# Attention into a feed-forward block on one core: blocks that follow the batches, and loads moved to GpSimd's queue

## The chip, the cores and the metric

The kernel runs on one core of one Trainium2 chip. The metric is device time in microseconds (us) of one execution. A core has five engines with a queue each: TensorE (PE: matmuls, and PEld for its weight loads), VectorE (DVE), ScalarE (ACT), GpSimd (POOL) and SyncE (SP, which only issues DMAs here). Each engine takes its queue in order.

## The reference

```python
def phi(x):
    proj = np.einsum('bhsd,df->bhsf', x, w_phi)
    proj = proj - np.max(np.abs(proj), axis=-1, keepdims=True)
    return np.concatenate([np.exp(proj), np.exp(-proj)], axis=-1)
q_p, k_p = phi(q), phi(k)                       # q, k, v: 8 batches, 8 heads, 576 tokens, 64
kv = np.einsum('bhsf,bhsd->bhfd', k_p, v)
num = np.einsum('bhsf,bhfd->bhsd', q_p, kv)
den = np.einsum('bhsf,bhf->bhs', q_p, k_p.sum(2))[..., None] + 1e-6
x = (num / den).transpose(0, 2, 1, 3).reshape(8 * 576, 512)
h = x @ w_in                                    # 512 x 2048
out = (h * erf(softplus(h))) @ w_out            # 2048 x 512
```

## The kernel before

The attention is done for pairs of heads, four pairs a batch, 32 in all (`NPAIR`, `B`), in groups of four tiles of 128 tokens (`GT`). A group goes through `k_piece` (projection in `project`, L500, maximum and subtraction on DVE in `front`, L468, Exp on ACT), `t_piece` (q is turned, from pair 8 on by a DMA transpose in `turn`, L566: DVE copies to `pl`, SP issues `plt<-pl`, DVE copies back, ACT takes two Exps), `kv_piece` (L576) and `n_piece` (L607). `n_tile` (L612) divides and writes x as two halves of float16 into a tile `xt`: VectorE makes `xf`, ACT or DVE casts it (`XT_ACT`), and POOL or DVE subtracts to get the low half (L651, `X_POOL`). One `xt` holds two pairs, that is half of a batch's channels.

`x_piece` (L692) then turns `xt` by DMA transposes on SP's queue (L704) into tiles `x` of 256 tokens by 512 channels (named `big` in the profile). The 4608 tokens are cut into 18 blocks of 256 (`TB`, `NBLK`), and since a batch has 576 tokens, most blocks hold parts of two batches: a piece of 128 tokens is often cut in two at the edge of a block. This makes 96 transposes.

The feed-forward part takes a block in two halves of the 2048 hidden columns. `h_chunk` (L764) multiplies `x` by `w_in`, with both in a high and a low float16 half, so three matmuls each; `erf_gate` (L799) runs on ACT and DVE; `o_chunk` (L823) multiplies by `w_out`. The first four blocks (`FIRST`) are taken over the first hidden half and then over the second, with partial sums kept in DRAM (`part`). `load_weight` (L408) brings 32 pieces of the weights (512 KB each) to `big` tiles, from where four DVE operations and one of ACT make the two halves (L427 to L436). `load_pair` (L441) brings q and k of a pair into one of three tiles `ld`. All these loads, `v`, the transposes, the partial sums and the output are issued by SP.

The order of each engine's queue is no loop of the program: every operation is recorded in a `Plan` with an assumed cost, due place and buffers, `Plan.run` (L174) lays them out on the five engines, and each queue is then issued in that order. Where the plan sees PE idle for over 600 ns (`HOLE`) it puts in filler matmuls of a tile `hot` (L958). So a constant or a cost in the plan changes the order on all engines, and what the chip does beside it is settled by semaphores.

## Time and profile before

| | |
|---|---|
| median of 3 runs | 995.19 us (995.09 to 996.29) |
| the profiled execution | 995.3 us, span of its instructions 993.5 us |
| granted TensorE clock | 1.0 |
| PE busy | 982.7 us, 99% of the span |
| ACT, DVE, POOL busy | 667.2, 631.3, 56.2 us |
| DMA | 85.94 MB, of the share below nearly all on the queue of SP |

The page gives the busy time of each engine over the span. Busy time of PE is from the start of a matmul to its modelled end, and matmuls overlap, so a short wait can hide under the end of the one before. The views used below are: the waits (who waited for whom), stretches (busy time of each engine in a window), the timeline (instructions in order of time; an entry of SP is the time in which it issues, and in brackets stands the idle time ahead and what ended it), and the view of one tile.

### The profile page before, as it was taken

The numbers are of one execution on the slowest core, as the hardware profiler recorded it, in microseconds if no ns is written. First come the engines' busy times: TensorE is split into PE (matmuls) and PEld (weight loads), VectorE is DVE, ScalarE is ACT, GpSimd is POOL, SyncE is SP. The second block draws the span as 40 slices with busy tenths as digits, with TensorE's granted clock in tenths as the row PEclk, the third lists the DMA queues.
The fourth block names the chain that finished last, engine by engine and source line by source line (L and its number), as shares of the span: only waits on it lengthen the run. The fifth ranks groups of instructions, "written<-read, shape, count | busy, mean of one in ns | idle before, by whom it ended". The sixth has DMA issues, their size and how long they took to land.

```text
span 993.5 us, 36288 instructions
## 1 busy us (share of the span) xinstructions
PE 982.7 (99%) x16674; PEld 780.1 (79%) x16674; DVE 631.3 (64%) x1140; ACT 667.2 (67%) x930; POOL 56.2 (6%) x70
## 2 busy tenths in 40 slices
PE   9999989999999999999999999999999999999998
PEld 7897678777788878877778887878778887777774
DVE  6999989996487826665627775578737742123322
ACT  7869759877667757667657667666857655566571
POOL 0201330210110100000000000000000000000000
PEclk9999999999999999999999999999999999999999
DMA  7492495553344242141313353224232120000000
GB/s 289 125 300 95 123 234 135 142 159 87 83 117 118 48 78 63 45 115 38 81 26 66 74 109 84 72 71 95 66 63 48 34 61 12 13 23 2 22 13 32
DMA packets 118713, 85.94 MB, mean 86 GB/s; under 512 B 99360, under 2 KB 99488, under 8 KB 118560
## 3 DMA queue, kind: packets, MB, share of 16 engines
q1 hardware_dynamic: 118560, 83.62, 32.9%
q8 instruction: 130, 2.13, 0.9%
q14 instruction: 23, 0.19, 0.1%
HBM read 48.46 MB, written 11.53 MB: 60 GB/s over the span
## 4 chain that ended last, share of the span: by engine, by line
PE 87%; ACT 6%; DVE 4%; DMA 1%; issue 1%; SPq 0%; DVEq 0%; ACTq 0%
PE bank L379 69%; PE bank L389 12%; PE bank L523 5%; ACT big L397 1%; DMA plt<-pl 1%; ACT big L794 1%; DVE m L471 1%; PE bank L554 1%; PE bank L958 1%; ACT gh L818 1%; DVE half L431 1%; ACT big L783 1%; ACT L809 1%; ACT L794 1%; DMA big<-in_moe_w_in_dram 0%
## 5 line engine op out<-in xcount | busy, mean ns | idle before, releaser
L379 PE MATMUL bank<-big,wih 128*64 128x256 f16 x4608 | 390.0, 273 | 2.8 <-DMA big<-xt 2.2
L379 PE MATMUL bank<-big,wil 128*64 128x256 f16 x2304 | 318.8, 273 | 0.2 <-DVE wil L435 0.2
L379 PEld LDWEIGHTS <-wih 128*64 128x64 f16 x4608 | 256.6, 110 | 29.1 <-DMA big<-xt 1.9
L397 ACT ACTIVATE big<-big 128x512 f32<-128x512 f32 x234 | 146.3, 629 | 125.0 <-DVE big L482 67.9
L379 PE MATMUL bank<-wol,gh 128*64 128x512 f16 x1152 | 220.6, 379 | 0.0
L379 PE MATMUL bank<-woh,gl 128*64 128x512 f16 x1152 | 220.4, 379 | 0.0
L379 PE MATMUL bank<-woh,gh 128*64 128x512 f16 x1152 | 220.4, 380 | 0.0
L379 PEld LDWEIGHTS <-gh 128*64 128x64 f16 x2304 | 128.8, 110 | 87.0 <-issue 0.3
L783 ACT ACTIVATE big<-bank 128x512 f32<-128x512 f32 x144 | 84.9, 591 | 146.5 <-PE bank L379 146.3
L815 DVE TENSOR_TENSOR big<-big,big 128x1024 f32<-128x1024 f32 x72 | 85.7, 1224 | 152.6 <-ACT big L811 152.5
L379 PEld LDWEIGHTS <-wil 128*64 128x64 f16 x2304 | 131.4, 110 | 2.2 <-DVE wil L435 0.5
L379 PEld LDWEIGHTS <-gl 128*64 128x64 f16 x1152 | 65.4, 110 | 56.3 <-DVE dn L626 0.2
L819 DVE TENSOR_TENSOR gl<-big,gh 128x1024 f16<-128x1024 f32 x72 | 87.3, 1222 | 23.8 <-ACT gh L818 23.7
L471 DVE TENSOR_REDUCE m<-bank 128x4 f32<-128x512 f32 x144 | 92.6, 681 | 12.6 <-PE bank L523 12.0
L389 PE MATMUL bank<-kv,big 128*64 128x65 f32 x2304 | 84.0, 222 | 0.6 <-DVE kv L600 0.6
L389 PEld LDWEIGHTS bank<-v,big 128*64 128x64 f32 x2016 | 75.1, 137 | 9.3 <-ACT big L397 2.9
L389 PE MATMUL bank<-v,big 128*64 128x65 f32 (+1 forms) x2016 | 80.2, 228 | 2.0 <-ACT big L397 1.8
L389 PEld LDWEIGHTS bank<-kv,big 128*64 128x64 f32 x2304 | 76.8, 138 | 4.1 <-issue 1.2
L818 ACT CAST gh<-big 128x1024 f16<-128x1024 f32 x72 | 74.1, 1037 | 0.2
L794 ACT ACTIVATE big<-big 128x1024 f32<-128x1024 f32 x72 | 72.6, 1049 | 0.4
L856 DVE TENSOR_SCALAR half<-bank 128x512 f32<-128x512 f32 x28 | 19.2, 685 | 58.7 <-PE bank L379 58.7
L571 DVE COPY big<-plt 128x1024 uint16<-128x1024 uint16 x54 | 42.3, 783 | 17.8 <-DMA plt<-pl 17.5
(54 smaller groups left out, 916.0 us busy)
## 6 DMA issues: line engine op xcount, KB each, us to landing
ld<-in_qk_dram SPq DMA_DIRECT2D x31, 576.0 KB, 4.7
out_dram<-half SPq DMA_DIRECT2D x36, 256.0 KB, 2.2
v<-in_vp_dram SPq DMA_DIRECT2D x28, 325.0 KB, 3.8
big<-in_moe_w_in_dram SPq DMA_DIRECT2D x16, 512.0 KB, 6.2
big<-in_moe_w_out_dram SPq DMA_DIRECT2D x16, 512.0 KB, 5.0
part<-half SPq DMA_DIRECT2D x8, 256.0 KB, 3.6
half<-part SPq DMA_DIRECT2D x8, 256.0 KB, 3.2
big<-xt SPq DMA_TRANSPOSE x96, 3.0
```

Source lines behind the costliest of these rows:

```text
L379: nc.tensor.matmul(o[half], a[:, half], b, start=start, stop=stop)
L389: nc.tensor.matmul(o[half], a[:, half], b, start=first and c == 0, stop=last and c == 1)
L397: nc.scalar.activation(out_(), in_(), func, **k)
L471: op(DVE, 600, lambda: nc.vector.tensor_reduce(m.t, ps(), axis=AX.X, op=ALU.max, apply_absolute_value=True), r=[b], w=[m])
L523: nc.tensor.matmul(both[nm].t[:, t * P : (t + 1) * P], x()[rows], w.t[rows, :], start=i == 0, stop=i == len(terms) - 1)
L571: op(DVE, 640, lambda: nc.vector.tensor_copy(qview(qp)[:, 1, :].bitcast(U16).rearrange("p (n h) -> p h n", h=2), turned.t.rearrange("p (h ...
L783: o = op(ACT, 490, lambda: nc.scalar.activation(h.t[:, q * 512 : (q + 1) * 512], b.t, AF.Copy, scale=SG / (SX * SWI)), r=[b], w=[(h, q)])
L794: fn = lambda: nc.scalar.activation(L.t, h.t, AF.Softplus, scale=1.0 / SG)
L815: op(DVE, 1140, lambda h=h, L=L: nc.vector.tensor_tensor(h.t, h.t, L.t, op=ALU.mult), r=[L, h], w=[h], port=True, off=GATE_OFF[0] * (v + 1))
L818: op(ACT, 940, lambda h=h, a=a: nc.scalar.copy(a.t, h.t), r=[h], w=[a], off=GATE_OFF[1] * (v + 1))
L819: op(DVE, 1140, lambda h=h, a=a, b=b: nc.vector.tensor_tensor(b.t, h.t, a.t, op=ALU.subtract), r=[h, a], w=[b], port=True, off=GATE_OFF[2] ...
L856: op(DVE, 600, lambda: nc.vector.tensor_scalar_mul(s.t, b.t, scale), r=[b], w=[s])
```

## The change

Blocks: 16 of the 18 blocks are now tokens 0 to 255 and 256 to 511 of a batch, and the last 64 tokens of four batches make one block (`blocks`, `REST`). `x_piece` issues three transposes for each half of a batch (two of 256 tokens, one of 64): 48 in place of 96, of the same bytes. The moving operand of `h_chunk` is then two runs of 128 columns (`moving`) where it was one of 256. The last chunk of the output is made in two halves of 256 columns (`split_chunk`), with two stores each; the other stores of the two tail blocks are halved by rows.

Queues: q and k of pairs 4 to 31 (28 loads) and weights 8 to 31 (24 loads) are issued by GpSimd. The plan's constants that go with it: more buffers for `x` and `qp`, casts of pairs 8 to 11 on ACT, subtractions of pairs 12 to 15 on DVE, the copies of `kv` of pairs 1 to 7 on ACT (before, 0 to 5), weights asked for a little later, and more slack ahead of PE's early operations.

```diff
+REST = 4
+QK_POOL = 4, 32
+W_POOL = 8, 32
-X_POOL = 0, 16
+X_POOL = 0, 12
-XS = 5
+XS = 6
-W_EARLY = 6
+W_EARLY = 7
-W_NS2 = 7000.0
+W_NS2 = 9000.0
-KV_ACT = 0, 6
-XT_ACT = 0, 8
+KV_ACT = 1, 8
+XT_ACT = 0, 12
-W_EACH = 5
+W_EACH = 7
-SLACK0 = 300.0
+SLACK0 = 600.0
-QPS = 3
+QPS = 4
...
-        op(SP, 430, lambda: nc.sync.dma_start(st.t.bitcast(I32), src), w=[st], done=2500, land=2600*LAND)
+        q, eng = (POOL, nc.gpsimd) if W_POOL[0] <= i < W_POOL[1] else (SP, nc.sync)
+        op(q, 430 + 140 * (W_POOL[0] <= i < W_POOL[1]), lambda: eng.dma_start(st.t.bitcast(I32), src), w=[st], done=2500 + 1500 * (W_POOL[0] <= i < W_POOL[1]), land=2600*LAND)
...
+            q, eng = (POOL, nc.gpsimd) if QK_POOL[0] <= p < QK_POOL[1] else (SP, nc.sync)
+            op(q, 450 if p == 0 else 600, lambda c=c: eng.dma_start(t.t[:, c], qk[p, :, c]),
...
+    blocks = []
+    for b in range(B):
+        blocks += [(b, 0), (b, 1)] + ([(b // REST, 2)] if b % REST == REST - 1 else [])
...
+            if part == 2:
+                to = xhalf(dst, half)[:, i // 2 * 512 : i // 2 * 512 + 512].rearrange("p (c t) -> p c t", c=4)[:, :, i % 2 * 64 : i % 2 * 64 + 64]
+                src = x2.t[0:64, 0, :]
+            else:
+                to = xhalf(dst, half).rearrange("p (n t) -> p n t", t=P)
+                src = x2.t[:, 1 + 2 * part : 3 + 2 * part, :].rearrange("p j n -> p (j n)")
+            nc.sync.dma_start_transpose(to, src)
...
-            return [(x_piece, p // NPAIR, p // 2 % 2, j) for p in done for j in (1, 2, 3, 4, 0)]
+            return [(x_piece, p // NPAIR, p // 2 % 2, j) for p in done for j in range(3)]
...
+    def moving(x, cc, lo):
+        return xhalf(x, cc // 2).rearrange("p (j c t) -> p j c t", j=2, c=4)[:, :, 2 * lo + cc % 2, :]
...
+    def split_chunk(n, fq, b):
...
+        for e in range(2):
+            b = halves[n[0]][e]
+            cols = slice(e * 256, e * 256 + 256)
...
+            if n[1] and fq:
+                s = buf("osb")
+                op(DVE, 400, lambda b=b, s=s, cols=cols: nc.vector.tensor_scalar_mul(s.t[:, cols], b.t[:, 0:256], 1.0 / (SG * SWO)), r=[b], w=[s])
+                for i in range(2):
+                    r0, own = (g * REST + 2 + i) * S + 512, slice(64 * i, 64 * i + 64)
+                    op(SP, 400, lambda s=s, r0=r0, own=own, cols=cols: nc.sync.dma_start(out[r0 : r0 + 64, cols], s.t[own, cols]), r=[s], done=2400)
...
+        if blk == NBLK - 1 and tt == 1:
+            yield from split_chunk(n, fq, b)
+            return
```

The queue of SP at the place where x of the first half of batch 1 (tile `xt_144`) is turned; `part` are partial sums, `plt` the turned q, `ld` the tile of q and k, `half` the tiles of weights and partial sums. Before:

```order
L704 DMA_TRANSPOSE big_85<-xt_144 128x4x128
L704 DMA_TRANSPOSE big_85<-xt_144 128x4x64
L704 DMA_TRANSPOSE big_94<-xt_144 128x4x64
L704 DMA_TRANSPOSE big_94<-xt_144 128x4x128
L704 DMA_TRANSPOSE big_94<-xt_144 128x4x64
L704 DMA_TRANSPOSE big_92<-xt_144 128x4x64 x2
L861 DMA part_97<-half_106 128x512
L861 DMA part_98<-half_107 128x512
L570 DMA_TRANSPOSE plt_136<-pl_134 128x8x128
L444 DMA ld_118<-in_qk_dram 128x1152
L426 DMA big_84<-in_moe_w_in_dram 128x1024
```

And now:

```order
L712 DMA_TRANSPOSE big_85<-xt_144 128x4x64
L712 DMA_TRANSPOSE big_84<-xt_144 128x8x128
L712 DMA_TRANSPOSE big_93<-xt_144 128x8x128
L453 DMA v_121<-in_vp_dram 128x650
L900 DMA part_97<-half_106 128x512
L900 DMA part_98<-half_107 128x512
L887 DMA half_108<-part_97 128x512
L887 DMA half_106<-part_98 128x512
L575 DMA_TRANSPOSE plt_136<-pl_134 128x8x128
L575 DMA_TRANSPOSE plt_137<-pl_135 128x8x128
```

Three transposes stand where seven stood, and the loads of q and k and of weights have left the queue. The queue of POOL around the subtractions for the same tile, before:

```order
L651 TENSOR_TENSOR xt_144<-xf_142,xt_144 64x128
L651 TENSOR_TENSOR xt_144<-xf_143,xt_144 128x4x64
L651 TENSOR_TENSOR xt_144<-xf_142,xt_144 128x4x64
L651 TENSOR_TENSOR xt_144<-xf_143,xt_144 64x128
L651 TENSOR_TENSOR xt_144<-xf_142,xt_144 128x4x64
L496 TENSOR_TENSOR ld_117<-ld_119,ld_117 128x640
L651 TENSOR_TENSOR xt_144<-xf_143,xt_144 128x4x64
```

And now, from the second subtraction on:

```order
L656 TENSOR_TENSOR xt_144<-xf_143,xt_144 128x4x64
L430 DMA big_92<-in_moe_w_out_dram 128x1024
L430 DMA big_91<-in_moe_w_out_dram 128x1024
L430 DMA big_93<-in_moe_w_out_dram 128x1024
L430 DMA big_89<-in_moe_w_out_dram 128x1024
L430 DMA big_86<-in_moe_w_out_dram 128x1024
L656 TENSOR_TENSOR xt_144<-xf_142,xt_144 128x4x64
L656 TENSOR_TENSOR xt_144<-xf_143,xt_144 64x128
L656 TENSOR_TENSOR xt_144<-xf_142,xt_144 128x4x64
L501 TENSOR_TENSOR ld_117<-ld_119,ld_117 128x640
L430 DMA big_91<-in_moe_w_in_dram 128x1024
L449 DMA ld_118<-in_qk_dram 128x1152
```

Five loads of weights now stand between two subtractions of one tile, and more behind them; each waits for a free tile before it is issued, and POOL does nothing else meanwhile.

## Rows read from the trace of the kernel before

**Rows 1.** The page: the span, and PE over the whole of it.

```profile
span 993.5 us, 36288 instructions
...
PE 982.7 (99%) x16674; PEld 780.1 (79%) x16674; DVE 631.3 (64%) x1140; ACT 667.2 (67%) x930; POOL 56.2 (6%) x70
```

**Rows 2.** Stretches: length, then busy us (count) by engine, PE's clock, DMA share, GB/s.

```profile
40.00:105.00 65.00, 64.61 (x1224) 54.79 (x1220) 62.55 (x122) 52.51 (x88) 9.40 (x13) 1.00 0.54 167
...
120.00:135.00 15.00, 11.82 (x240) 8.62 (x234) 12.04 (x21) 7.66 (x14) 4.03 (x4) 1.00 1.18 269
...
135.00:140.00 5.00, 3.80 (x70) 3.90 (x72) 4.82 (x10) 2.89 (x5) 1.98 (x1) 1.00 0.49 118
...
135.00:200.00 65.00, 63.02 (x1204) 55.31 (x1206) 60.85 (x109) 52.81 (x73) 13.78 (x14) 1.00 0.61 155
200.00:805.00 605.00, 605.00 (x10588) 483.65 (x10584) 398.10 (x736) 404.87 (x522) 16.17 (x20) 1.00 0.33 76
```

**Rows 3.** The waits of PE: whom it waited for, us in total, times, longest.

```profile
PE bank L379 <- DMA big<-xt: 2.2, 1, 2.2
PE bank L389 <- ACT big L397: 1.8, 3, 1.3
```

**Rows 4.** Timeline of SP from 105 to 138 us: start, us, instruction.

```profile
105.44 9.74 SPq L704 DMA_TRANSPOSE big<-xt  x7
...
118.85 0.64 SPq L444 DMA_DIRECT2D ld<-in_qk_dram  x1
...
122.51 3.75 SPq L570 DMA_TRANSPOSE plt<-pl  x1
...
129.51 8.30 SPq L704 DMA_TRANSPOSE big<-xt  x6
```

**Rows 5.** Timeline of ACT and of DVE where they wait for these DMAs.

```profile
123.67 1.24 ACT L493 CAST ld<-ld 128x640 f16<-128x640 f32 x2 [3.51 <-DMA ld<-in_qk_dram]
...
131.46 0.75 DVE L571 COPY big<-plt 128x1024 uint16<-128x1024 uint16 x1 [2.82 <-DMA plt<-pl]
```

**Rows 6.** Views of tiles and of a line: issue ns (min/median/max), time to landing.

```profile
L704 SPq DMA_TRANSPOSE big<-xt x96: 1169/1256/3030, 38.3 to 814.4; - x96
...
L570 SPq DMA_TRANSPOSE plt<-pl x54: 1231/1236/3752, 117.4 to 796.8; - x54
...
DMA to landing us min/median/max: 3.0/3.1/8.9
```

**Rows 7.** Timeline of PE: eight pairs over 512 columns, and pairs over 256.

```profile
120.54 0.39 PE L379 MATMUL bank<-woh,gl 128*64 128x512 f16 x2
...
122.05 0.39 PE L379 MATMUL bank<-woh,gh 128*64 128x512 f16 x2
...
136.20 0.41 PE L379 MATMUL bank<-big,wih 128*64 128x256 f16 x4 [2.15 <-DMA big<-xt]
...
139.80 0.41 PE L379 MATMUL bank<-big,wih 128*64 128x256 f16 x4
```

**Rows 8.** Timeline of PE: a stretch of four pairs of fillers.

```profile
50.70 1.05 PE L958 MATMUL bank<-hot 128*64 128x512 f16 x8
```

**Rows 9.** The end: timeline of DVE, the stores, DVE on half a tile.

```profile
989.71 0.69 DVE L856 TENSOR_SCALAR half<-bank 128x512 f32<-128x512 f32 x1 [1.90 <-PE bank L379]
...
L858 SPq DMA_DIRECT2D out_dram<-half x36: 332/343/1092, 245.7 to 990.4; - x36
...
L643 DVE TENSOR_TENSOR xf<-bank,dn 128x256 f32<-128x256 f32 x64 | 27.0, 421 | 2.0
```

**Rows 10.** POOL: its subtractions in all, two in the timeline, and a load's issue on SP.

```profile
L651 POOL TENSOR_TENSOR xt<-xf,xt x48: 418/667/1516, 25.8 to 347.7; 128x256 f16<-128x256 f32 x32, 64x128 f16<-64x128 f32 x16
...
104.62 0.67 POOL L651 TENSOR_TENSOR xt<-xf,xt 128x256 f16<-128x256 f32 x1 [13.31 <-ACT xt L646]
...
112.18 1.21 POOL L651 TENSOR_TENSOR xt<-xf,xt 128x256 f16<-128x256 f32 x1 [1.61 <-ACT xt L646]
...
L426 SPq DMA_DIRECT2D big<-in_moe_w_in_dram x16: 327/428/580, 7.4 to 145.1; - x16
```

More of the change, by code (lines that the diff above doesn't have):

```diff
@@ L569, in turn @@
             parts.t, u.t.rearrange("p t f -> p (t f)").bitcast(U16).rearrange("p (n h) -> p h n", h=2)), r=[u], w=[parts], port=True)
-        op(SP, 1280, lambda: nc.sync.dma_start_transpose(turned.t, parts.t.rearrange("p h n -> p (h n)")), r=[parts], w=[turned], done=4700)
+        op(SP, 1280, lambda: nc.sync.dma_start_transpose(turned.t, parts.t.rearrange("p h n -> p (h n)")), r=[parts], w=[turned], done=4700, land=600)
         op(DVE, 640, lambda: nc.vector.tensor_copy(
@@ L678, in favor_attention_moe @@
     xs = {}
-    def xview(x, half):
-        return x.t.bitcast(F16)[:, half * HW : (half + 1) * HW].rearrange("p (c t) -> p c t", c=4)
-    def x_reads(blk, half):
-        return [(xs[blk], (half, t)) for t in {max(t, blk * TB) - blk * TB for b in range(B) for j in range(5)
-                for t in piece(b, j, blk)}]
-    def piece(b, j, blk):
-        t0 = b * S + ((j - 1) * P if j else 512)
-        e0 = t0 + (P if j else 64)
-        return [t0] if t0 < (blk + 1) * TB and e0 > blk * TB else []
@@ L692, in x_piece @@
-    def x_piece(b, half, j):
-        n = P if j else 64
-        t0 = b * S + ((j - 1) * P if j else 512)
-        t = t0
-        x2 = xt[2 * b + half]
-        keys = [(x2, (r, k, i)) for r in range(2) for k in (("tail",) if j == 0 else (0, 1)) for i in range(2)]
-        while t < t0 + n:
-            blk = t // TB
-            e = min(t0 + n, (blk + 1) * TB)
-            if blk not in xs:
-                xs[blk] = buf("x")
-            dst = xs[blk]
-            op(SP, 1280, lambda dst=dst, t=t, e=e, blk=blk: nc.sync.dma_start_transpose(
-                xview(dst, half)[:, :, t - blk * TB : e - blk * TB], x2.t[t - t0 : e - t0, j, :]),
-               r=keys, w=[(dst, (half, t - blk * TB))], done=3400 if b == 0 else 2900, land=100)
-            t = e
+    blocks = []
@@ new lines, in favor_attention_moe, with xhalf, x_piece, fn @@
+    for b in range(B):
+        blocks += [(b, 0), (b, 1)] + ([(b // REST, 2)] if b % REST == REST - 1 else [])
+    def xhalf(x, half):
+        return x.t.bitcast(F16)[:, half * HW : (half + 1) * HW]
+    def x_reads(blk, half):
+        g, part = blocks[blk]
+        return [(xs[blk], (half, i)) for i in (range(REST) if part == 2 else [0])]
+    def x_piece(b, half, part):
+        x2 = xt[2 * b + half]
+        keys = [(x2, (r, k, i)) for r in range(2) for k in (("tail",) if part == 2 else (0, 1)) for i in range(2)]
+        blk = blocks.index((b // REST, 2) if part == 2 else (b, part))
+        if blk not in xs:
+            xs[blk] = buf("x")
+        dst = xs[blk]
+        i = b % REST
+        def fn():
+            if part == 2:
[5 more added lines that the diff above has]
+            nc.sync.dma_start_transpose(to, src)
+        op(SP, 1280, fn, r=keys, w=[(dst, (half, i if part == 2 else 0))], done=3400 if b == 0 else 3100, land=250 if part == 2 else 600)
@@ L777, in h_chunk @@
                 for i, (w, lo) in enumerate(((wih, 0), (wih, 1), (wil, 0))):
-                    mm(109, lambda k=k, cc=cc, fs=fs, w=w, x=x, lo=lo: (ps()[:, k, :], w.t[:, cc, fs], xview(x, cc // 2)[:, 2 * lo + cc % 2, :]),
+                    mm(109, lambda k=k, cc=cc, fs=fs, w=w, x=x, lo=lo: (ps()[:, k], w.t[:, cc, fs], moving(x, cc, lo)),
                        [(w, key), *x_reads(blk, cc // 2)], [b], cc == 0 and i == 0, cc == NCC - 1 and i == 2)
@@ L843, in o_chunk @@
             return
-        r0 = blk * TB + tt * P
+        g, part = blocks[blk]
+        rows = [(g * S + part * TB + tt * P, slice(0, P))]
+        if part == 2:
+            rows = [((g * REST + 2 * tt + i) * S + 512, slice(64 * i, 64 * i + 64)) for i in range(2)]
         scale = 1.0 / (SG * SWO)
@@ L857, in o_chunk @@
         if half:
-            op(SP, 400, lambda: nc.sync.dma_start(out[r0 : r0 + P, :], s.t), r=[s], done=2400, land=1300*LAND)
+            for r0, own in rows:
+                op(SP, 400, lambda r0=r0, own=own: nc.sync.dma_start(out[r0 : r0 + own.stop - own.start, :], s.t[own, :]), r=[s], done=2400, land=1300*LAND/len(rows))
         else:
@@ L925, in pe_time @@
         return 10400.0 * ((h is not None) + (o is not None))
-    starts = [next(i for i, (h, _) in enumerate(steps) if h == ((b * S) // TB, 0)) for b in range(1, B)]
+    starts = [next(i for i, (h, _) in enumerate(steps) if h == (blocks.index((b, 0)), 0)) for b in range(1, B)]
     owed = since = 0.0
```

15 lines of the change are left out of this document (12 added, 3 removed).

## The prediction

> **What bounds the kernel now.** The page comes first: PE is busy for 982.7 of 993.5 us [rows 1]. A faster kernel needs less work on PE, or less idle time of PE, and there is little of it. The stretches say where it lies [rows 2]: from 200 to 805 us PE is busy for 605.00 of 605.00 us, so nothing that another engine or a queue does better there is worth anything. Before that, PE idles 0.39 us of 40 to 105, then 3.18 us of 120 to 135 and 1.20 us of 135 to 140, and another 0.78 us up to 200 (63.02 of 65 with the 1.20 taken off). That is 5.55 us in all, 4.38 of it within 120 to 140.
>
> The waits of PE name what ended this time [rows 3]: 2.2 us for x, which a DMA transpose brings (`big<-xt`), and 1.8 us for an Exp of ACT (`big` L397). The timeline of SP tells why both come late [rows 4]. From 105.44 SP issues seven transposes of x in a row, 9.74 us. Only then do the load of q and k (118.85) and a turned q (122.51, whose issue took 3.75 us) go out, and all land together: the DMA share is 1.18 from 120 to 135 [rows 2]. ACT stands for 3.51 us until that q and k are there, and DVE for 2.82 us until that turned q is there [rows 5]; it took 8.9 us to land where the median is 3.1 [rows 6]. Then six more transposes follow, from 129.51, 8.30 us [rows 4], and PE's matmul of a new block waits 2.15 us for them, to 136.20 [rows 7]. So the loss is one burst: SP's queue, filled by transposes, lets loads out late and in a heap.
>
> **The change, part by part.** *PE's work.* The number of feed-forward columns is the same: 96 matmuls of 512 columns become 192 of 256. A pair over 512 columns takes (122.05 - 120.54)/7 = 216 ns, one over 256 (139.80 - 136.20)/33 = 109 ns [rows 7], so 48 pairs of the one and 96 of the other both take 10.4 us: 0. The queue of PE now holds 46 fillers where it held 42, two pairs more; four pairs took 1.05 us [rows 8], so **+0.5 us**. They stand for places where the plan sees PE without work, so they may cost nothing on top of that; I keep the 0.5.
>
> *The moving operand in two runs.* No row of before has one. All 3456 pairs of `h_chunk` are touched, so a small price counts. Nothing excludes a cost, and there is no reason for a gain (the columns are as many). From the two pair times, a pair costs 3 ns beside its columns (2 x 109 - 216 = 2, rounded up). If each run paid that once, 3456 x 3 ns = 10.4 us: the bounds are 0 and 10.4. I take 0, since doubling the columns from 256 to 512 adds no more than their time, so a column costs the same wherever it stands; the upper end is a rival below.
>
> *Transposes.* 96 become 48. One issue takes 1.256 us, and a `plt` of the size that the merged ones have takes 1.236 us [rows 6], so SP is free of some 48 x 1.25 = 60 us of issue. Outside the burst this is worth 0, for PE has no idle time there [rows 2]. In it, the seven of 9.74 us become three, about 3.8 us, and the six that PE waited for become three. Also a block of a batch now needs no piece of the batch before.
>
> *The loads on GpSimd's queue.* 24 loads of weights (0.43 us each to issue on SP [rows 10]) and 28 of q and k leave SP, so the q and k that was out at 118.85 no longer stands behind transposes. On POOL they wait for a free tile, and what stands behind them there is the subtractions for x (and so the transposes, and so PE). What they cost on POOL no row shows. The lower end is SP's 0.43 us. For the upper end I take the longest subtraction of x, 1.5 us [rows 10], as POOL's work, plus a wait of the same length: 3 us. By the new order of POOL's queue 35 of them stand ahead of the last three subtractions for batch 2, so before about 230 us. POOL is busy for 56.2 us in all [rows 1], 16.17 of them from 200 to 805 [rows 2], so 40 before 200; with 35 x 0.43 = 15 us more it is far from full, with 35 x 3 = 105 us it is busy for some 145 of 200. I take a price near the lower end, since most of these loads come where POOL is idle: 13.31 us ahead of the subtraction at 104.62 [rows 10], where five loads now stand. The cost is then 0, covered by that idle time.
>
> *The other constants.* Casts and subtractions that change hands are some 4 us of DVE and ACT work after 200 us, where these are busy for 398 and 405 of 605 us [rows 2]: 0. *The end.* The last operation of DVE covers 256 columns, 0.42 us where it took 0.69, and behind it stand two stores where one stood, 0.34 us more to issue [rows 9]: -0.27 + 0.34, about 0.
>
> **The sum** goes against the profiled execution, 995.3 us, of which 993.5 are the span; it stands 0.1 above the median of the runs, so no correction is made. The burst goes: -4.38. Two pairs of fillers: +0.5. The 1.17 us of idle time elsewhere stays, as nothing here is aimed at it. 995.3 - 4.4 + 0.5 = **991.4 us**.
>
> **The rivals.** *A: the transfers, not the queue.* The DMA share of 1.18 [rows 2] can be read so that the engines that move the bytes were full, and not SP's queue late. The bytes are the same, and x, turned q, q and k and weights of batch 1 are still wanted within the same 20 us. Then the heap forms again, and PE loses its 4.4 us at this place or the next: 995.3 + 0.5 = 995.8 us, no difference. For it speaks that a turned q took 8.9 us to land where 3.1 is usual [rows 6]; against it, that the share is 0.54 from 40 to 105, so there is room to send earlier what SP's queue held back. The Trainium skill, page "DMA: Bandwidth & Descriptors", section "Issuing engines are not separate DMA queues", states this rule: transfers from all queues run on the same 16 engines, and more queues only save the time of issue. By that rule the landing times would not gain here; the trace agrees with it as far as the share goes, and speaks for the time of issue with the 9.74 us.
>
> *B: GpSimd becomes the queue that is late.* At 3 us a load POOL is nearly full, and it takes its queue in order. Ahead of the subtraction at 112.18 it idled for 1.61 us only [rows 10], and now four loads stand shortly before it: 12 us for 1.61 us of room. x of batch 1 would be late by up to 10 us, less the 6 us that the transposes save; the 4.4 us would be lost as before, and the next two batches, whose weights also stand between subtractions, would lose the 2.15 us of [rows 7] each: 995.3 + 0.5 + 4.3 = 1000.1 us, slower. It decides from about 2.5 us a load. For it speaks that POOL's subtraction takes 667 ns at the median but up to 1516 [rows 10], while DVE is busy for 62.55 of 65 us [rows 2], so something holds POOL up beside a busy DVE; against it, the 13.31 us of idle time. The Trainium skill, page "SBUF — State Buffer", section "SBUF: two separate sides", warns of this: a DMA from GpSimd has its descriptors written by GpSimd, and DVE in some modes locks it out meanwhile; its section "A bandwidth-pool intuition that's wrong (but worth ruling out)" gives 620 ns for one alone and 3100 ns beside a copy on DVE. By that figure, as an estimate, a load would cost what B needs. No run here shows it yet.
>
> *C: the two runs cost 3 ns a pair:* 991.4 + 10.4 = 1001.8 us.
>
> **How the numbers follow.** A measurement of this kernel can tell about 0.2%, 2.0 us: faster is below 993.2, slower above 997.2. I give the forecast 0.56 (the cause is seen in three engines at one place, and the orders show it gone), A 0.25, B 0.15, C 0.04. So faster 0.56, same 0.25, slower 0.15 + 0.04 = 0.19. The likeliest case alone runs from 989 (all 5.55 us of idle time go, and fillers cost nothing on top) to 993.2. The range must take in A and the nearer half of B; it starts at 988.5 for waits that hide under the end of a matmul, and ends at 998.5, between A and B. Left out are about half of B, C and a little below: 0.16.
>
> **What would show it.** Right: in the stretch in which batch 1's x is turned, SP issues three transposes of about 1.25 us in a row; PE idles for under 1 us there; ACT and DVE do not wait for `ld` or `plt`; a load on POOL takes under 1.5 us; pairs of `h_chunk` keep their 109 ns; 605 of 605 us stay busy in the middle. Wrong in the way of A: `plt<-pl` again lands in 6 us or more beside a share near 1. Wrong in the way of B: POOL busy for over 100 us in the first 200, and PE waiting for `big<-xt` at the first block of batches 1 to 3. Wrong in the way of C: 112 ns a pair.

## The result, and the profile after

The changed kernel takes **998.24 us** (median of 20 runs, 994.03 to 1004.55). The kernel before, run beside it, takes 996.58 us (median of 20, 994.61 to 999.27). The ratio is **1.0024, 95% interval 1.0013 to 1.0036**: slightly slower, where 991.4 us and faster had been forecast. Its runs also spread over 10.5 us where those of before spread over 4.7. Two single executions that took far longer than all others of their kernel (1124.96 us of the kernel before, 3660.61 us in one experiment) are left out of the ratios below. The first profiled execution took 996.47 us, 1.8 us less than the median; its span is 1.2 us longer than that of before:

```profile
span 994.7 us, 36435 instructions
...
PE 984.1 (99%) x16774; PEld 789.1 (79%) x16774; DVE 626.5 (63%) x1140; ACT 672.1 (68%) x943; POOL 79.2 (8%) x110
```

The stretches of [rows 2], in the changed kernel (length, then busy us and count of PE, PEld, DVE, ACT and POOL, PE's granted clock, DMA share, GB/s):

```profile
40.00:105.00 65.00, 64.16 (x1200) 54.66 (x1199) 61.47 (x122) 53.64 (x90) 16.36 (x26) 1.00 0.55 173
120.00:135.00 15.00, 12.57 (x246) 9.93 (x244) 13.13 (x25) 10.43 (x18) 7.15 (x8) 0.95 0.97 198
135.00:140.00 5.00, 5.00 (x80) 5.00 (x77) 1.99 (x3) 1.75 (x3) 2.50 (x4) 0.81 0.97 260
135.00:200.00 65.00, 63.81 (x1212) 55.82 (x1209) 54.97 (x95) 52.83 (x79) 17.85 (x23) 0.99 0.58 149
200.00:805.00 605.00, 604.62 (x10586) 484.78 (x10582) 401.63 (x751) 405.93 (x523) 22.18 (x28) 1.00 0.33 76
```

From 120 to 140 us PE now idles 2.43 us where it idled 4.38. But the stretches beside it gave some back: 0.84 us from 40 to 105 (before 0.39), 1.19 from 135 to 200 (all of it after 140, where before had 0.78), 0.38 from 200 to 805 (before 0). In all, 4.84 us of idle time where there were 5.55. In this execution the place of the burst is still the worst one. The waits of PE (in total, times, longest):

```profile
PE bank L382 <- DMA big<-xt: 2.4, 1, 2.4
PE bank L382 <- ACT wih L400: 0.9, 1, 0.9
```

This is the same wait as in [rows 3], for x of batch 1. The timeline of SP's queue before it (start, us of issue):

```profile
121.19 1.21 SPq L712 DMA_TRANSPOSE big<-xt  x1
...
125.58 2.72 SPq L712 DMA_TRANSPOSE big<-xt  x2
128.41 7.03 SPq L575 DMA_TRANSPOSE plt<-pl  x2
```

So SP's queue is short now: three transposes of some 1.3 us, where [rows 4] had seven and then six. But it is not free: the two turned q's behind them took 7.03 us to issue, where the median of one is 1.24 in this trace. At the same moment the timeline of POOL has

```profile
125.50 0.79 POOL L449 DMA_DIRECT2D ld<-in_qk_dram  x1
126.28 0.68 POOL L430 DMA_DIRECT2D big<-in_moe_w_in_dram  x1
```

and the DMA view of 125 to 129 us (KB each, median us from issue to landing) says what this did to the transposes:

```profile
ld<-in_qk_dram POOLq DMA_DIRECT2D x1, 576.0 KB, 5.9
big<-in_moe_w_in_dram POOLq DMA_DIRECT2D x1, 512.0 KB, 7.3
big<-xt SPq DMA_TRANSPOSE x2, 8.6
plt<-pl SPq DMA_TRANSPOSE x1, 8.3
```

They land after 8.6 us; before, the six of the same place, which were smaller, took 4.1 us at the median in the same view. A closer match is the experiment below with all loads on SP's queue, where the same two take 6.1 us (view of 124 to 128 us). Then PE's own timeline, with one more thing in it:

```profile
133.78 0.64 PE L382 MATMUL bank<-big,wih 128*64 128x256 f16 x4 [2.43 <-DMA big<-xt]
...
134.37 0.69 PE L382 MATMUL bank<-big,wih 128*64 128x256 f16 x4
...
136.91 0.41 PE L382 MATMUL bank<-big,wih 128*64 128x256 f16 x4
...
137.23 0.41 PE L382 MATMUL bank<-big,wih 128*64 128x256 f16 x4
```

From 136.91 to 137.23 three pairs take 0.32 us, 107 ns each, as in [rows 7]. But right after the wait, from 133.78 to 136.91, three pairs take 0.64 us, twice as long (134.37 is the second group of them). The stretch from 133.8 to 136.8, with PE busy throughout, says why: the granted clock is 0.50, the lower of the two levels, 1.2 GHz.

```profile
133.80:136.80 3.00, 3.00 (x30) 3.00 (x31) 0.07 (x1) 0.60 (x1) 2.70 (x5) 0.50 1.19 164
```

In 3.1 us at half the clock PE lost about 1.6 us that count as busy time. In before, the wait of 2.15 us at this place brought no such fall [rows 7]. So in this execution, of the 4.38 us that should have gone, 1.95 went, 1.6 were lost to the clock and 1.24 to idle time elsewhere (0.45 + 0.41 + 0.38); that makes +0.9. The last store also comes later: from DVE's last operation to the end of the span there are 994.7 - 990.42 = 4.3 us, before 993.5 - 989.71 = 3.8 [rows 9]. With this +0.5 it is +1.4, near the measured 1.2.

```profile
990.42 0.42 DVE L850 TENSOR_SCALAR half<-bank 128x256 f32<-128x256 f32 x1 [0.88 <-PE bank L382]
```

A second profiled execution of the same kernel took 998.43 us, close to the median, and lost its time at another place. Two of its stretches and three waits of PE:

```profile
120.00:140.00 20.00, 18.95 (x381) 16.47 (x378) 13.95 (x25) 14.43 (x25) 9.26 (x11) 1.00 0.97 230
140.00:200.00 60.00, 53.35 (x1009) 44.85 (x1006) 50.86 (x89) 46.24 (x69) 14.75 (x18) 1.00 0.52 122
...
PE bank L382 <- ACT big L793: 2.7, 1, 2.7
PE bank L382 <- ACT wih L400: 1.9, 1, 1.9
...
PE bank L382 <- DMA big<-xt: 0.9, 1, 0.9
```

Here PE idles 1.05 us from 120 to 140, where before had 4.38, but 6.65 us from 140 to 200, where before had 0.78, and mostly for ACT. The granted clock is 1.00 in every stretch. With 0.57 us from 40 to 105 and 0.35 from 200 to 805 that makes 8.62 us of idle time for 5.55, or +3.1; the span is 996.7 - 993.5 = 3.2 us longer. So the long wait for x and the fall of the clock belong to the first execution and not to every one. What both have in common is that the idle time which left the place of the burst came back at others.

And what the loads cost POOL, from the views of their lines (issue ns min/median/max):

```profile
L430 POOL DMA_DIRECT2D big<-in_moe_w_out_dram x16: 530/530/778, 54.2 to 210.9; - x16
...
L430 POOL DMA_DIRECT2D big<-in_moe_w_in_dram x8: 530/553/890, 92.3 to 136.7; - x8
...
L449 POOL DMA_DIRECT2D ld<-in_qk_dram x28: 530/574/786, 17.3 to 717.8; - x28
```

### The profile page after: what moved, and what is told of

The parts are those of the page before. It is cut to its first block, busy times and chain, and to the rows that moved or that the text cites. A ratio compares the mean times of both kernels' runs of the same rounds, so it can differ in the third digit from the quotient of the medians.

```text
span 994.7 us, 36435 instructions
## 1 busy us (share of the span) xinstructions
PE 984.1 (99%) x16774; PEld 789.1 (79%) x16774; DVE 626.5 (63%) x1140; ACT 672.1 (68%) x943; POOL 79.2 (8%) x110
## 3 DMA queue, kind: packets, MB, share of 16 engines
q8 instruction: 131, 2.15, 0.9%
## 4 chain that ended last, share of the span: by engine, by line
PE 88%; DVE 5%; ACT 4%; DMA 1%; issue 1%; SPq 0%; DVEq 0%
PE bank L382 68%; PE bank L392 13%; PE bank L528 5%; PE bank L559 1%; DVE m L476 1%; PE bank L997 1%; DVE big L576 1%; ACT big L804 1%; DMA part<-half 1%; DMA plt<-pl 1%; ACT big L400 0%; ACT gh L828 0%; DVE pl L573 0%; DVE half L433 0%; DVE big L487 0%
## 5 line engine op out<-in xcount | busy, mean ns | idle before, releaser
L382 PE MATMUL bank<-woh,gh 128*64 128x512 f16 (+1 forms) x1184 | 223.5, 374 | 0.4 <-ACT woh L400 0.4
L382 PE MATMUL bank<-woh,gl 128*64 128x512 f16 (+1 forms) x1184 | 223.7, 374 | 0.0
L382 PE MATMUL bank<-wol,gh 128*64 128x512 f16 (+1 forms) x1184 | 223.5, 373 | 0.0
L382 PEld LDWEIGHTS <-gh 128*64 128x64 f16 x2368 | 133.3, 110 | 82.5 <-issue 0.7
L382 PEld LDWEIGHTS <-gl 128*64 128x64 f16 x1184 | 67.8, 110 | 54.4 <-DVE dn L631 0.2
L449 POOL DMA_DIRECT2D ld<-in_qk_dram x28 | 16.1, 577 | 473.3 <-DVE ld L501 273.0
```

Of the source, the lines that this page charges most:

```text
L382: nc.tensor.matmul(o[half], a[:, half], b, start=start, stop=stop)
L449: op(q, 450 if p == 0 else 600, lambda c=c: eng.dma_start(t.t[:, c], qk[p, :, c]), w=[(t, c.start)], done=2300 + 1500 * (QK_POOL[0] <= p < ...
```

## The experiments

Each ratio is to runs of the kernel before on the same chip; those had medians of 996.2 to 997.0 us. The edits are shown against the changed kernel, or against the kernel before where the text says so. The expectations name their theories by letters. T: a second queue lets bulk loads out beside the transposes that PE waits for, and so delays them. G: GpSimd itself is late, by the price of issuing loads or by late subtractions. K, in the first run: the slower executions are those in which the granted clock falls (in the run with 7000 and both queues K is another theory, on the spacing). R, in the later runs: ACT has no room in the first 200 us and holds PE once the burst is gone.

### Which part costs: one queue at a time

The changed kernel once more, without an edit:

> The changed kernel as it is, for a second profile and more times. Theory T (transfers): the wait of PE for the first new block of batch 1 is not gone because q and k and a weight, now in a queue of their own, share the transfer engines with the two transposes of x that PE waits for; it should be there again, 2 to 5 us, with transposes of x landing in over 6 us near 126 us. Theory G (GpSimd late): in a slower execution the loads on GpSimd take over 1 us each to issue and its subtractions come late. Theory K (clock): slower executions are those in which the granted clock falls after that wait. Times as before, 994 to 1004, wider than those of the kernel before.

Measured: 997.6 us (994.22 to 1007.58), ratio 1.0020 [1.0000, 1.0041]. The result holds, and so does its spread. The wait that T expected here, 2 to 5 us, is 0.94 us in this execution (the second one shown above), although the two transposes of x again land late, after 7.7 us. G gets no support: the loads on GpSimd issue in 527 to 778 ns. Nor does K: this execution took 998.43 us at a granted clock of 1.00, and the longest of the first 20 runs, 1004.55 us, also ran at 1.00 throughout.

All loads on SP's queue, blocks and constants kept:

```diff
-QK_POOL = 4, 32
-W_POOL = 8, 32
+QK_POOL = 0, 0
+W_POOL = 0, 0
```

> The change without the move of the loads: all loads on SP, the new blocks and all other constants kept. T: with one queue the transposes go ahead of loads that are issued later, so the blocks alone should give 0 to 4 us (992 to 997) and a narrower spread than the change. G: the same direction, since GpSimd has no loads. If the new blocks themselves cost (two runs of columns, other constants), it stays at 997 to 1000 or above.

Measured: 995.58 us (993.96 to 996.64), ratio 0.9992 [0.9984, 1.0001]. Without the second queue the kernel is 2 to 3 us better than the changed one, and its spread is 2.7 us; but it gains nothing on before that these runs can tell. The wait for x is nearly gone (0.3 us); the waits of PE are now

```profile
PE bank L382 <- ACT big L793: 1.9, 1, 1.9
PE bank L382 <- ACT wih L400: 1.9, 1, 1.9
```

for ACT, at 158 and 177 us. These are the two waits of the second execution above, with one queue. So the burst can be taken away, and something else comes late.

Only the weights back on SP's queue (`W_POOL = 0, 0`):

> Only q and k of pairs 4 to 31 on GpSimd's queue, the weights on SP. T: half of the second stream is gone, time between the two others, 994 to 998. G: GpSimd is free of 24 of 52 loads, so most of the loss and of the spread should go.

Measured: 996.35 us (995.1 to 997.71), ratio 1.0003 [0.9994, 1.0012]. The loads of q and k on GpSimd's queue cost 0.8 us against all on SP's, or nothing, since the intervals overlap.

Only q and k back on SP's queue (`QK_POOL = 0, 0`), so the weights alone on GpSimd's:

> Only weights 8 to 31 on GpSimd's queue, q and k on SP. T: weights beside the transposes, 995 to 1000. G: the loads that stand in rows between the subtractions remain, so the loss and the spread remain.

Measured: 1009.44 us (1004.51 to 1013.09), ratio **1.0127 [1.0102, 1.0152]**. The weights on GpSimd's queue cost 13 us by themselves, more than with the loads of q and k in the same queue, and far more than T's 995 to 1000 us. Against the kernel with all loads on SP's queue this is the cleanest pair of all runs: in both traces the operations of PE, DVE and ACT stand in the same order from start to end, by the names of their tiles, and what differs is the queue of 24 loads. From 40 to 105 us, all loads on SP's queue first, then the weights on GpSimd's:

```profile
40.00:105.00 65.00, 64.42 (x1220) 55.00 (x1217) 61.76 (x123) 54.02 (x91) 9.11 (x13) 1.00 0.56 171
...
40.00:105.00 65.00, 60.43 (x1124) 53.39 (x1120) 56.20 (x113) 47.97 (x81) 14.87 (x23) 0.95 0.54 169
```

G does not explain it: the weights issue in 0.55 and 0.57 us at the median and 0.78 at most, and POOL's subtractions take 668 ns at the median in both. The timeline of POOL, the DMA view of 49 to 52 us and PE's timeline show one of its places:

```profile
49.32 1.75 POOL L430 DMA_DIRECT2D big<-in_moe_w_out_dram  x3
```

```profile
big<-in_moe_w_out_dram POOLq DMA_DIRECT2D x3, 512.0 KB, 7.7
big<-xt SPq DMA_TRANSPOSE x2, 8.8
```

```profile
57.96 0.64 PE L382 MATMUL bank<-big,wih 128*64 128x256 f16 x4 [4.57 <-DMA big<-xt]
```

Three weights of the second matmul, wanted much later, go out together beside two transposes of x that PE waits for, and these land after 8.8 us, where the same two land after 3.6 us with all loads on SP's queue; PE waits 4.57 us and then takes 0.64 us for three pairs, half the clock. The mean granted clock of this execution is 0.992 over 1010.4 us, that of the other 0.999 over 993.9 us; so some 0.007 x 1010 = 7 of the 16.5 us between the two are time at the lower clock. In the changed kernel the load of q and k that stands ahead of these weights in POOL's queue waits for a free tile, which holds them back until the transposes are out. So the loads of q and k hid part of what the weights cost.

### Holding the weights back

The same kernel as the last, but the first weight of `w_out` (16) waits until x of blocks 0 and 1 has landed: two tiny copies on POOL read the landed x into a tile that the load names as read.

```diff
...
+            for n, (xb, k) in enumerate(xr):
+                op(POOL, 150, lambda gt=gt, xb=xb, n=n: nc.gpsimd.tensor_copy(gt.t[:, 4 * n : 4 * n + 4], xhalf(xb, 1)[:, 0:4]), r=[(xb, k)], w=[(gt, n)])
+                held.append((gt, n))
...
```

> The kernel with only the weights on GpSimd's queue (1009.4 us), and ahead of the first weight there two tiny copies on GpSimd that read the tiles which the transposes of batch 0 bring, so that this weight and those behind it go out only when these have landed. T: the 4.6 us wait of PE near 53 us (transposes landing in 8.5 and 9.1 us beside three weights), and the granted clock of 0.5 for 6.8 us behind it (3.4 us lost), go; 998 to 1003. If the loss comes from GpSimd's queue itself (issue cost, subtractions late), it stays at 1007 or more.

Measured: 1004.4 us (1003.76 to 1007.02), ratio 1.0085 [1.0068, 1.0101]. About 4 of the 13 us come back with one gate, less than T expected (998 to 1003 us) and more than G (1007 or more). At the gate T holds: from 40 to 105 us PE idles 1.34 us where it idled 4.57, at a clock of 1.00. But PE still waits 4.15 us for x of batch 1 (132.8 to 136.9 us), where no gate stands.

The changed kernel with this gate, and one on weight 12 for blocks 2 and 3:

> The changed kernel with the same two copies ahead of the first weight on GpSimd, and two more ahead of the weight that was issued at 126.28 us, which read x of batch 1. T: transposes of x near 126 us land in under 7 us, PE waits under 1.5 us for them, and slow executions (over 1000) become rare: 995 to 998, spread under 5 us. If the spread stays at 994 to 1007, it is not these two weights that make it.

Measured: 998.93 us (997.3 to 1003.58), ratio 1.0029 [1.0016, 1.0041]: no gain, outside T's 995 to 998 us, and the spread is 6.3 us. The wait for x is down to 0.8 us, and PE's longest wait, 2.8 us, is now at 157 us and for ACT. So a gate takes away one collision, and the wait for ACT takes its place; whether the gates also hold up what stands behind them on POOL was not measured.

### What holds the head of the kernel

All loads on SP's queue, both `Erf` of ACT over 256 of 1024 columns:

> Blocks as in the change, all loads on SP (995.6 us), and both Erf operations of each step over 256 of 1024 columns, in the same order of all queues: Erf is left out for three quarters of the columns, about 1.5 us less of ACT in each of 36 steps. Theory R (room on ACT): with transposes out of the way PE waits for ACT near 158 and 177 us, where ACT runs without a gap from 148 to 180; then these waits (about 4 us) go, and the end of the last step is 1 to 2 us shorter: 989 to 992. If the waits are transfers or VectorE, it gains no more than the 1 to 2 us at the end: 993.5 to 995.

Measured: 994.06 us (992.98 to 995.51), ratio 0.9980 [0.9970, 0.9989].

All loads on SP's queue, two of DVE's four operations for a weight over 64 of 512 columns:

> The same kernel with all loads on SP, and two of VectorE's operations for each weight over 64 of 512 columns (the bits of seven eighths of the weights are left incomplete): 1.1 us less of VectorE for each of 32 weights, all before 240 us, in the same order. If VectorE is what holds PE up in the head (it is busy there for 94% and more), the waits go: 990 to 992. R: ACT stays the bound and the waits near 158 and 177 stay: 994.5 to 996.

Measured: 992.18 us (990.73 to 994.15), ratio 0.9963 [0.9951, 0.9976]. Against the same kernel uncut (0.9992) ACT's cut gains 1.2 us and DVE's 2.9. R as it was put fails: by it ACT's cut should have given 989 to 992 us, and DVE's should have left 994.5 to 996. With less work on DVE both waits for ACT go (at most 0.2 us is left), and PE idles 0.20 us from 140 to 200 where it idled 4.38; with less work on ACT they fall from 1.9 and 1.9 to 0.8 and 0.7 us. DVE's time lies just above the 990 to 992 that were expected if DVE holds PE. So on the new blocks with SP's queue it is mainly DVE's work that sets when these pieces are ready, ACT's in part.

The kernel before, with the same cut of DVE's work:

> The kernel before with two of VectorE's four operations for each weight over 64 of 512 columns (the rest of these columns is left uncomputed, so the weights are not the reference's). If the burst of SP's queue bounds the head of the kernel before, as the prediction said, VectorE's 30 us of work less change little: 994 to 996 us, and the waits of 2.15 us at 134 us and 2.8 us of VectorE for the turned q stay. If VectorE's work sets when everything in the head is wanted and ready, it gains what the same cut gained on the other blocks, 3 to 4 us: 991 to 993 us.

Measured: 995.42 us (median of 11, 992.73 to 997.19), ratio 0.9990 [0.9980, 1.0000]. The same cut gains about a third of that here. In the profiled execution, the fastest of them, the wait for x goes, against the expectation that it stays if the burst binds; but the wait for an `Exp` of ACT before 125.3 us is 1.77 us where it was 1.30, and behind it the granted clock is 0.50 from 127.3 to 130.5 us. So less work on DVE is not enough on the blocks of before; that burst and DVE bind together there is a reading that no run settles.

### The parts alone on the kernel before

The queues alone (against before, with the code that these two switch):

```diff
+QK_POOL = 4, 32
+W_POOL = 8, 32
```

> The kernel before, with q and k of pairs 4 to 31 and weights 8 to 31 on GpSimd's queue and nothing else changed (its blocks of 256 tokens, 96 transposes and constants stay). Theory T (a second queue lets bulk loads out beside the transposes that TensorE waits for, so it costs time): 998 to 1004 us, and the waits of TensorE for x at the first blocks of batches 1 and 2 grow beyond 2.2 us. Theory Q of the prediction (loads leave a queue that is full of transposes, and that helps): 992 to 994 us. If only the blocks interact badly with the queues, it stays at 995 to 997 us.

Measured: 1011.21 us (1008.21 to 1013.9), ratio **1.0142 [1.0124, 1.0160]**. The blocks, the transposes and the constants are those of before. The order is not quite: the plan counts 140 ns more for a load on GpSimd and 1500 ns more until it is there, and from about 33 us on the operations of PE, DVE and ACT stand in another order. Part of the 14.6 us may come from that; the pair above, at 13 us, is free of it. The DMA view of before from 53 to 60 us, all on SP's queue:

```profile
big<-in_moe_w_out_dram SPq DMA_DIRECT2D x2, 512.0 KB, 6.0
...
big<-in_moe_w_in_dram SPq DMA_DIRECT2D x1, 512.0 KB, 4.7
...
big<-xt SPq DMA_TRANSPOSE x2, 3.1
```

There the two transposes are issued at 53.48, the weight of the first matmul at 56.72, and the weights of the second behind that. With two queues, from 53 to 58 us:

```profile
big<-in_moe_w_out_dram POOLq DMA_DIRECT2D x3, 512.0 KB, 7.3
ld<-in_qk_dram POOLq DMA_DIRECT2D x1, 576.0 KB, 5.2
big<-in_moe_w_in_dram SPq DMA_DIRECT2D x1, 512.0 KB, 8.7
...
big<-xt SPq DMA_TRANSPOSE x2, 9.9
```

The weights of the second matmul, wanted last, and a load of q and k go out beside the transposes and land before them; the transposes take 9.9 us for 3.1, and the weight of the first matmul 8.7 for 4.7. PE then waits for that weight, and at 137 us for x:

```profile
PE bank L381 <- DMA big<-xt: 4.5, 1, 4.5
PE bank L381 <- DVE wil L438: 4.4, 1, 4.4
```

The blocks alone: all loads on SP's queue, and the plan's constants as before.

> The blocks that follow the batches and 48 transposes alone: all loads on SP's queue and the plan's constants as they were before. If the constants (weights asked for later, casts and copies moved to ScalarE) brought the waits for ScalarE near 158 and 177 us that the kernel with all loads on SP showed, this one is at 992 to 994 us and lacks those waits. If VectorE and ScalarE are simply full in the first 200 us, whatever the constants, it stays at 995 to 997 us, with a wait of 1 to 3 us for one of them in that stretch.

Measured: 996.45 us (994.92 to 997.32), ratio 0.9997 [0.9989, 1.0006]. Half as many transposes, by themselves, are worth nothing that these runs can tell: PE waits 1.4 us for x and 1.9 us for ACT's half of a weight at 177 us.

The queues on before, with the changed kernel's constants of the weights (`W_NS2 = 9000.0`, `W_EACH = 7`, `W_EARLY = 7`):

> The kernel before with the loads on GpSimd's queue and the changed kernel's constants of the weights (9000 ns, a weight in seven, seven loaded early); its blocks stay. Theory S: the cost of the queue falls from 14.6 us to 2 to 6 us (998 to 1003 us). Theory B2 (blocks with 96 transposes suffer from the second queue whatever the spacing, the new blocks less): 1006 to 1012 us.

Measured: 1019.21 us (1012.47 to 1020.82), ratio 1.0219 [1.0194, 1.0243]. Worse, outside either expectation. In its DMA view of 53 to 62 us four weights and again a load of q and k of GpSimd's queue stand beside the same two transposes, and these land after 14.4 us. So two transposes landed after 3.1 and 3.6 us beside no load of GpSimd's queue, after 8.8 beside three weights, after 9.9 beside three weights and a q and k, and after 14.4 beside four and a q and k.

### The spacing of the weights

All loads on SP's queue, and weights 16 to 31 asked for as densely as before:

```diff
-W_NS2 = 9000.0
+W_NS2 = 7000.0
```

> The new blocks and constants with all loads on SP's queue, and weights spaced as they were before in the plan (7000 for 9000 ns). The wait for a weight's high half near 177 us (2.0 us) should go if the spacing made it late: 993 to 994.5 us. If ScalarE is late by its own queue (it ran without a gap from 148 to 180 us), the wait stays or moves: 995 to 996.5 us.

Measured: 993.56 us (992.76 to 995.5), ratio 0.9968 [0.9956, 0.9981]; and on another chip

> The new blocks with all loads on SP's queue and 7000 ns, a second time, to see whether its gain holds on another chip: 993 to 994.5 us, 0.2 to 0.4% below the kernel before. If the first time was chance, 995 to 996.5 us.

994.48 us (993.62 to 997.11), ratio 0.9982 [0.9973, 0.9992]. Against the kernel before that is 1.8 to 3.2 us; against the same kernel with 9000 (0.9992) it is 1.0 to 2.4 us, from a constant for which the sum of the prediction had no term. The wait for ACT near 177 us is 1.1 us where it was 1.9.

The same with `W_NS2 = 5000.0`:

> The same with 5000 ns. If the late high halves of the weights near 176 us (1.1 us of wait left at 7000) are a matter of when the loads are asked for, 992 to 993.5 us, and that wait is under 0.5 us. If they are a matter of ScalarE's and VectorE's time, no gain over 7000: 993.5 to 996 us.

Measured: **992.8 us** (991.72 to 995.9), ratio 0.9966 [0.9956, 0.9976]. PE's waits, but for 1.5 us at the very start, are down to

```profile
PE bank L382 <- ACT big L793: 0.9, 1, 0.9
PE bank L382 <- DMA big<-xt: 0.7, 1, 0.7
PE bank L382 <- issue: 0.3, 1, 0.3
```

and PE is busy for all of the 605 us from 200 to 805. The wait for ACT's half of a weight near 176 us is gone, so it was a matter of when the loads were asked for. A shorter spacing is no remedy in itself, as the kernel before with 5000 shows:

> The kernel before with weights 16 to 31 asked for at a spacing of 5000 ns in the plan, nothing else. If the spacing alone is what made the new blocks with all loads on SP's queue 0.3% faster, this one gains the same: 992.5 to 994 us. If the gain needs the new blocks (48 transposes), the burst of transposes near 130 us stays with its wait of 2 us for x, and the time is 995.5 to 997.5 us.

Measured: 1005.11 us (1004.5 to 1007.25), ratio 1.0089 [1.0071, 1.0107], a miss for both readings. Its longest wait stands in the old place,

```profile
132.08 2.00 PE L389 MATMUL bank<-kv,big 128*64 128x65 f32 x32 [4.13 <-DVE kv L600]
```

and the copy of `kv` is late because DVE, which takes its queue in order, stood for 3.60 us ahead of it, at 128.50, for a turned q. That is not all: the plan put in 76 filler matmuls where before has 42, 17 pairs more, some 4.5 us of PE's time by [rows 8], and the granted clock is 0.86 from 120 to 135 and 0.75 from 135 to 140 us, some 3.4 us. PE is busy for 989.5 us, 6.8 more than in before. So the gain of 5000 needs the new blocks, or the other constants that came with them; which of the two was not tried.

The changed kernel, both queues kept, with 7000:

> The changed kernel with weights 16 to 31 spaced in the plan as they were before (7000 for 9000 ns); its queues stay. Theory S (the wider spacing holds the second queue's weights back from the transposes and so hides most of what the queue costs): 1000 to 1008 us, with TensorE waiting for x or for a weight before 150 us longer than the 2.4 us of the changed kernel. Theory K (the spacing makes those weights late whatever queue they are in, as it did with all loads on SP's queue, where 7000 gave 2 us): 995.5 to 997 us, below the changed kernel.

Measured: 1007.37 us (1003.83 to 1011.36), ratio 1.0113 [1.0088, 1.0138]. On the new blocks the wide spacing is what hides most of the queue's cost: at 7000, both queues against one cost 13 to 14.5 us (1.0113 against 0.9968 and 0.9982; the operations of PE, DVE and ACT again stand in the same order), at 9000 about 3. On the old blocks it did not, as shown above; so this holds for one order of the queues and is no rule.

Last, the new blocks with 5000, q and k on GpSimd's queue and the weights on SP's:

> The new blocks with 5000 ns and only q and k of pairs 4 to 31 on GpSimd's queue; weights on SP's. If loads of q and k on a second queue are harmless (with 9000 ns they cost 0.8 us), 992.5 to 994 us, like all on SP's queue. If any second stream of loads delays the transposes here, TensorE waits for x again near 130 us and the time is 995 to 999 us.

Measured: **992.67 us** (991.58 to 993.19), ratio **0.9955 [0.9941, 0.9970]**, with no run above 993.19. The loads of q and k do no harm on GpSimd's queue that these runs can tell; with all loads on SP's queue the time is the same within the intervals. SP issues three weights behind the transposes, not beside them:

```profile
128.76 4.03 SPq L712 DMA_TRANSPOSE big<-xt  x2
132.89 1.26 SPq L575 DMA_TRANSPOSE plt<-pl  x1
134.20 1.54 SPq L430 DMA_DIRECT2D big<-in_moe_w_in_dram  x3
```

and the transposes issued from 123 to 131 us land after 5.1 us at the median, where the changed kernel's took 8.6.

The ratios by blocks, spacing and queue (without the gates and the light kernels; the new blocks have the changed kernel's other constants, except where it says otherwise):

| blocks | spacing of weights | all on SP | q, k on GpSimd | weights on GpSimd | both |
|---|---|---|---|---|---|
| old | 7000 | 1 | | | 1.0142 |
| old | 9000 | | | | 1.0219 |
| old | 5000 | 1.0089 | | | |
| new | 9000 | 0.9992 | 1.0003 | 1.0127 | 1.0024, 1.0020 |
| new | 7000 | 0.9968, 0.9982; with all constants of before 0.9997 | | | 1.0113 |
| new | 5000 | 0.9966 | 0.9955 | | |

## Why the prediction was wrong, step by step

*PE's work, the two runs, the fillers: right.* Pairs of `h_chunk` take 107 ns in the stretch shown, as before; rival C is out. Of the +0.5 for the fillers nothing is seen: the other terms of the first execution already give +1.4 for 1.2.

*SP's queue: right in the order, not in the time.* Three transposes of some 1.3 us stand where seven and six stood, and the loads no longer stand behind them. But SP was not free for it: the next two turned q's took 7.03 us to issue.

*A load's price on POOL: right, and near the lower end that was taken.* The medians are 530, 553 and 574 ns, the longest 890, with DVE busy for 61.47 of 65 us beside them. POOL is busy for 57 of the first 200 us, not for over 100; rival B is out as it was put. The Trainium skill, page "SBUF — State Buffer", section "A bandwidth-pool intuition that's wrong (but worth ruling out)", gives 620 ns for a DMA from GpSimd alone and 3100 ns beside a copy on DVE; the times of issue here, 530 to 890 ns, are near the first, and none is near the second.

*The burst goes, -4.38, and the idle time elsewhere stays: this step failed.* It took the place of an instruction in SP's queue for the whole cause, and PE as free once the burst is gone. The forecast is 991.4 / 995.3 = 0.9961 of the kernel before, the measurement 1.0024. The kernel with all loads on SP's queue, 0.9992, divides the difference: 3.1 us are lost without the second queue, 3.2 us by it. Three things came in place of the gain, each with its run:

1. The transfers collide from two queues as well. The heap formed again at 125 to 137 us, as rival A said: a turned q landed in 8.3 us beside a share of 0.97, DVE stood for 3.22 us until a turned q was there, and ACT for 1.50 us until q and k were. By the rule that was weighed there (page "DMA: Bandwidth & Descriptors" of the Trainium skill, "Issuing engines are not separate DMA queues") transfers of all queues interleave on the same 16 engines; the trace agrees that the landing times did not gain: the same two transposes land after 6.1 us with all loads on SP's queue and after 8.6 with two queues.
2. The second queue costs more than it saves. The sum priced the loads on GpSimd's queue at 0, covered by POOL's idle time, and that is so for POOL. But one queue also kept an order: transposes first, weights that are wanted later behind them. With two queues the weights go out beside the transposes, and at the places shown these land in 8 to 14 us where 3.1 was usual. The weights alone in that queue cost 13 us on the new blocks, with the order of PE, DVE and ACT unchanged. Rival A, "no difference", was thus too kind: the sign against the change was in the queue that it added, and no rival had it.
3. "The other constants: 0" was worked out for casts and subtractions alone; the spacing of the weights was put at nothing without a reason. With all loads on SP's queue 9000 for 7000 ns costs 1.0 to 2.4 us, and 2.6 us against 5000 (0.9992 against 0.9966): it makes the halves of the weights late near 177 us, at a place where the trace of before gave no warning beyond 0.6 us. With both queues the same constant gains some 9 us (1.0024 for 1.0113).

*The idle time elsewhere* grew by 0.86 us before 200 (0.45 from 40 to 105, 0.41 from 140 to 200) and by 0.38 behind in the first execution. In the second, near the median, it grew by 5.9 us (6.65 for 0.78) from 140 to 200 alone, more than the 3.3 us that the place of the burst gave back. With the burst taken away and all loads on SP's queue PE idles 4.38 us there, for ACT, and the light kernels show that DVE's work above all, and ACT's, is what it runs into.

*A wait can cost more than its length.* The sum knew only idle time. Behind the wait of 2.43 us PE ran for some 3.1 us at the lower clock, 1.6 us more, which stand as busy time in every view but the granted clock. The second execution had a wait of 2.75 us and no such fall, so this is no fixed price.

*The number.* That 998.24 us lies inside the stated range, 988.5 to 998.5, is luck: the range was drawn for rivals A and B, and the measurement is the sum of larger effects that none of them had, a second queue of 13 to 14.5 us and a spacing that hides most of it. A slip of the working: with all 5.55 us of idle time gone the sum is 989.75, not 989.

The mechanism of the forecast itself, that the burst holds PE and that shorter queues give it back, is borne out in part: in the two best versions PE's wait for x falls to 0.7 us (all loads on SP's queue) and 1.2 us, and their ratios, 0.9966 and 0.9955, are those of the forecast, 0.9961. But the blocks alone gave 0.9997. The gain came with the new blocks, the other new constants, SP's queue for the weights and the shorter spacing together.

Not settled: the spread of the changed kernel. It comes with the weights on GpSimd's queue (10.5 us, and 2.6 and 2.7 with the weights on SP's queue at the same spacing), but no long execution was profiled. Which of the two profiled executions is the common case is not known either. Nor was it tried to keep the weights on GpSimd's queue with a gate at every block; two gates did not pay.

## What to carry to other kernels

A queue that is full may also be what keeps transfers in the right order. Before loads move to a second queue, ask which transfers with a near deadline they will overtake, and move rather those that wait for their own buffer (here q and k, at no cost that was seen), not large ones that are free to go at any time. And where the removed wait is the longest of several close ones, sum what the next engine leaves, and try the plan's constants again after the change, since those that suit one order can hide the gain of another.

## What the runs showed of the hardware that was not expected

- A DMA transpose lands late beside loads of another queue: two of them landed in 3.6 us with all loads on SP's queue, and in 8.8 us beside three loads of 512 KB on GpSimd's, with the order of PE, DVE and ACT the same. On the old blocks, where two landed in 3.1 us, it was 9.9 us beside three such loads and one of 576 KB, and 14.4 beside four and one of 576 KB.
- Issuing a DMA transpose holds SP up where the transfers are many: 7.03 us for two beside a DMA share of 0.97, where the median of one is 1.24.
- The granted clock falls to 0.50 behind a wait of 2.43 us and stays there for 3.1 us of full work; behind the wait of 2.15 us in the trace of before, of 1.89 us with all loads on SP's queue and of 2.75 us in the second execution of the changed kernel, it did not fall; but behind the 1.77 us of the kernel before with DVE's work cut it did. So the length of the wait alone does not tell it. Behind the 4.57 us of the kernel with the weights alone on GpSimd's queue PE ran as slowly.
- GpSimd issues a load in 0.53 to 0.57 us at the median where SP takes 0.43 [rows 10], and a DVE that is busy for 61.47 of 65 us did not stretch it beyond 0.89.
